# A prefetch distance of two groups for raw weights, a DRAM detour for w2, and a new order of gates, leftovers and background work

## The chip, the core and the metric

The kernel runs on one core of one Trainium2 chip. The metric is the device time of one execution in microseconds; the figure given for a kernel is the median of its runs. TensorE, VectorE (DVE), ScalarE (ACT) and GpSimd (POOL) each work through their own queue in order; nearly all DMAs are issued by SyncE (SP), whose queue is in order too.

## The reference

```python
x = delta_attention(q, k, v, beta)      # 4 batches, 8 heads, 768 steps, head size 48; gives x [3072, 384]
logits = x @ w_gate                     # [3072, 8]
P = np.exp(logits - logits.max())
for _ in range(8):                      # Sinkhorn: rows, then columns
    P /= P.sum(1, keepdims=True) + 1e-09
    P /= P.sum(0, keepdims=True) + 1e-09
    P *= N / E
for e in range(8):
    h = np.maximum(x @ w1[e], 0.0)      # w1 [8, 384, 1024], w2 [8, 1024, 384]
    out += P[:, e:e + 1] * (h @ w2[e])
h = out @ w_in                          # w_in [384, 2048] and w_out [2048, 384] arrive as 64-bit floats
result = (h * np.cos(h)) @ w_out
```

## The kernel before

Every large product is made of three TensorE passes over rounded high parts and low remainders (`hi` and `lo`; the low part is the subtraction source minus high part, on VectorE or GpSimd).

*Attention and expert 0.* 12 chunks (`tick`, orders written out by hand in `SEQ`) run the attention; between their steps `half()` runs pieces of expert 0 for the blocks of 512 tokens that are done. In the last three chunks every second step also pops one closure of `t_prog(0)`, which loads blocks of x from DRAM (`lds`), makes sums and differences of them (`ops` on GpSimd, `neg` on VectorE), splits them into high and low (`emit`) and stores them in `tsc`.

*Lead.* From line 1299 the first raw weights and the tiles T (sums of x, 15 of them, 512 KB each) are loaded, and a loop (L1340) alternates pieces of expert 0 with the lists in `lead` and with Sinkhorn steps (`sk_some`, 12 in all; each waits on TensorE for a matmul with ones and then runs some eight small VectorE operations). Six pieces of expert 0 are left over for group 0 (`LEFT`).

*Groups.* Experts 1 to 7 run in 56 calls of `group(n)`: two passes (p = 0, 1) over 1536 tokens each, 28 groups of 256 hidden columns to a pass. A group makes 6 hidden tiles of 128x512 (three token blocks, two column halves) with 15 products of three matmuls (`m`, L1425) over sums of x and sums of w1, and sums of the results (`copy` on ScalarE, L1430; `vadd` on VectorE, L1433). Five PSUM banks X, Z, A, B, C_ change roles from group to group. `relu` (ScalarE L155, then VectorE L156) writes a hidden tile. Six calls of `F()` in a group each pop one fill piece: 9 matmuls of the second layer (`seg_piece`, L149) of the pair of groups before; every fourth piece closes a token block, and the next `gates()` multiplies the three banks by the gate (VectorE, L1457) and adds them on GpSimd (L1458). `bg()` pops one closure of background work, from group 4 on: `t_prog(1)` for the second pass, then the conversion of w_in and w_out (`conv`, nine VectorE steps per slice; the next slice's load two steps before its use).

*Weights of a group.* `g_load(n + 1)` at the start of group n loads raw w1 into `wraw` (first pass), and `s_prep(n + 1)` returns seven lists that `go(0)` to `go(6)` run at set places: `q0`, `q1` make the sums on GpSimd, `hi` and `lo` split them, `g_load2` then loads w2 into the same 768 columns of `wraw`, `w2h` and `w2l` split it, and `store` writes the finished sums (1.9 MB) to `wss`. The second pass loads those from `wss` and needs raw w2 alone. The places in a group, by products and fill pieces:

```python
N0 N2 F gates go(0) bg N1 N4 bg F go(1) bg N3 gates CE b a bg CD F gates go(2) bg
DF EF CF F gates go(3) d c F gates go(4) bg e relu go(5) F gates bg go(6)
```

*End.* After group 55 eight fill pieces are left and run between the first three steps of the last network (`net_step`), whose weights are loaded into ten tiles `cw` that take the place of the tiles T.

## Time and profile before

| | us |
|---|---|
| median of 3 runs (2369.21 to 2374.89) | 2370.85 |
| the profiled execution's own time | 2375.54 |
| its span | 2373.8 |
| TensorE busy in it | 2141.5 (90%) |
| VectorE busy | 1416.0 (60%) |
| GpSimd busy | 939.2 (40%) |
| ScalarE busy | 864.3 (36%) |

The span runs from the first to the last instruction that the profiler saw. A busy time is the union of an engine's instructions. An engine's idle time is put to the instruction that ends it and to whatever released that instruction. The granted clock is TensorE's, 1.0 for 2.4 GHz and 0.5 for 1.2 GHz, averaged over a stretch.

### The profile page before, as it was taken

How to read it: one execution, taken by the hardware profiler on the slowest of the kernel's cores; microseconds unless marked ns; L12 is line 12 of the kernel's file. 1: busy time of each engine (PE TensorE's matmuls, PEld its weight loads, DVE VectorE, ACT ScalarE, POOL GpSimd, SP SyncE). 2: the span in 40 equal slices, each digit the busy share in tenths (PEclk: the TensorE clock that was granted, in tenths of full speed). 3: DMA queues.
4: the chain of work that ended last, by engine and by line, in shares of the span. 5: the costliest groups of instructions: out<-in, count | busy, mean ns of one | idle time of the engine just before them, and what ended most of it. 6: DMA issues, size and time to landing. Idle time of an engine off the chain costs nothing.

```text
span 2373.8 us, 39737 instructions
## 1 busy us (share of the span) xinstructions
PE 2141.5 (90%) x16148; PEld 1755.9 (74%) x16148; DVE 1416.0 (60%) x2226; ACT 864.3 (36%) x1436; POOL 939.2 (40%) x1034
## 2 busy tenths in 40 slices
PE   7899999778788888888897989999999999999999
PEld 6787877566666676666675767777777778999998
DVE  6665433745556666666674656666666546666665
ACT  3333322333333333333332322323333325666665
POOL 4576542244455333333343433233323333333332
PEclk6899999889999999999998999999999999999999
DMA  4433244443344343333337532433434344000000
GB/s 86 109 86 81 74 142 141 171 155 128 138 152 148 111 163 108 115 125 127 129 120 285 198 133 94 170 127 125 150 111 158 110 148 171 27 27 27 14 4 24
DMA packets 210294, 279.71 MB, mean 118 GB/s; under 512 B 85520, under 2 KB 165872, under 8 KB 210112
## 3 DMA queue, kind: packets, MB, share of 16 engines
q1 hardware_dynamic: 207280, 270.40, 34.5%
q0 software_dynamic: 1664, 6.49, 0.8%
q8 instruction: 126, 2.06, 0.3%
q10 hardware_dynamic: 1168, 0.30, 0.1%
q14 instruction: 56, 0.46, 0.1%
HBM read 176.11 MB, written 101.02 MB: 117 GB/s over the span
## 4 chain that ended last, share of the span: by engine, by line
PE 70%; DMA 10%; DVE 7%; POOL 5%; issue 3%; ACT 3%; SPq 2%; POOLq 0%; DVEq 0%; ACTq 0%
PE ps L149 26%; PE ps L1425 18%; PE ps L1689 8%; PE ps L1647 8%; DMA wraw<-in_moe_w_dram 7%; PE ps L137 4%; DVE cth L1457 1%; DMA tp<-in_moe_w_in_dram 1%; PE ps L311 1%; ACT mh L155 1%; POOL tp L1044 1%; DVE w2t L1265 1%; PE ps L279 1%; SPq L1258 1%; DVE ps L1433 1%
## 5 line engine op out<-in xcount | busy, mean ns | idle before, releaser
L149 PE MATMUL ps<-mh,w2t 128*128 128x512 f32 x3060 | 769.4, 396 | 35.5 <-DVE cth L1457 35.5
L1425 PE MATMUL ps<-T,w1t 128*128 128x512 f32 x2520 | 671.8, 408 | 142.9 <-ACT scr L1430 94.9
L149 PEld LDWEIGHTS ps<-mh,w2t 128*128 128x128 f32 x3060 | 572.3, 190 | 184.2 <-DVE cth L1457 68.7
L1425 PEld LDWEIGHTS ps<-T,w1t 128*128 128x128 f32 x2520 | 489.5, 197 | 273.5 <-ACT scr L1430 107.0
L1458 POOL TENSOR_TENSOR accp<-accp,cth 128x512 f32<-128x512 f32 x246 | 334.5, 1389 | 700.8 <-DVE cth L1457 700.8
L155 ACT ACTIVATE mh<-ps 128x512 fp32r<-128x512 f32 x340 | 202.4, 598 | 626.1 <-PE ps L1425 246.9
L156 DVE SCALAR_TENSOR_TENSOR mh<-ps,mh 128x512 fp32r<-128x512 f32 x340 | 228.6, 687 | 180.3 <-ACT mh L155 178.9
L1433 DVE TENSOR_TENSOR ps<-scr,ps 128x512 f32<-128x512 f32 x168 | 116.5, 693 | 260.4 <-ACT scr L1430 169.8
L1430 ACT ACTIVATE scr<-ps 128x512 f32<-128x512 f32 x224 | 133.4, 595 | 150.2 <-PE ps L1425 141.7
L1656 POOL TENSOR_SCALAR tp<-tp 128x512 f32<-128x512 f32 x92 | 90.8, 987 | 204.0 <-ACT tp L1655 204.0
L1457 DVE TENSOR_TENSOR cth<-ps,scr 128x512 f32<-128x512 f32 x246 | 154.0, 681 | 1.2 <-PE ps L149 1.2
L1670 DVE TENSOR_TENSOR tp<-tp,ps 128x512 f32<-128x512 f32 x96 | 66.1, 688 | 135.7 <-ACT tp L1669 135.7
L1433 DVE TENSOR_TENSOR scr<-ps,scr 128x512 f32<-128x512 f32 x112 | 76.9, 687 | 82.7 <-PE ps L1425 50.2
L137 PE MATMUL ps<-xb,w1t 128*128 128x512 f32 x432 | 116.8, 416 | 5.5 <-DVE h L156 4.1
L1249 ACT ACTIVATE w1t<-wraw 128x128 fp32r<-128x128 f32 (+2 forms) x84 | 46.7, 590 | 200.1 <-DMA wraw<-in_moe_w_dram 195.3
L149 PE MATMUL ps<-h,w2t 128*128 128x512 f32 x396 | 103.1, 407 | 0.0
L137 PEld LDWEIGHTS ps<-xb,w1t 128*128 128x128 f32 x432 | 80.6, 195 | 24.2 <-DVE h L156 4.2
L1238 POOL TENSOR_TENSOR wraw<-wraw 128x256 f32<-128x256 f32 x28 | 20.4, 728 | 195.3 <-DMA wraw<-in_moe_w_dram 180.1
L149 PEld LDWEIGHTS ps<-h,w2t 128*128 128x128 f32 x396 | 77.0, 197 | 16.9
L390 POOL TENSOR_TENSOR w1t<-w1t 128x30 f32<-128x30 f32 (+9 forms) x150 | 81.0, 540 | 11.8
L1647 PE MATMUL ps<-xx,cw 128*128 128x512 f32 x360 | 84.0, 390 | 0.0
L1252 DVE TENSOR_TENSOR w1t<-wraw,w1t 128x128 fp32r<-128x128 f32 (+2 forms) x84 | 82.4, 981 | 0.0
(280 smaller groups left out, 2819.6 us busy)
## 6 DMA issues: line engine op xcount, KB each, us to landing
wss<-w1t SPq DMA_DIRECT2D x56, 768.0 KB
w1t<-wss SPq DMA_DIRECT2D x56, 768.0 KB
wraw<-in_moe_w_dram SPq DMA_DIRECT2D x84, 384.0 KB
wsn<-tp SPq DMA_DIRECT2D x64, 192.0 KB
wss<-w1t SPq DMA_DIRECT2D x28, 384.0 KB
scr<-pts SPq DMA_DIRECT2D x42, 256.0 KB
w1t<-wss SPq DMA_DIRECT2D x28, 384.0 KB
xsc<-xb SPq DMA_DIRECT2D x24, 384.0 KB
```

The source lines that it names most:

```text
L137: nc.tensor.matmul(out=ps[:, :nn], lhsT=w[:, a, kk, fs], rhs=x[:, b, kk, c0:c0 + nn], start=(i == 0), stop=(i == 3 * KD - 1),)
L149: nc.tensor.matmul(out=banks[kd], lhsT=w[:, a, f % 2, kd * 128:(kd + 1) * 128], rhs=h[:, b, :], start=(first and b == 0 and a == 0), stop= ...
L155: nc.scalar.activation(out=h[:, 0, :nn], in_=ps[:, :nn], func=ACTF.Relu)
L156: nc.vector.scalar_tensor_tensor(out=h[:, 1, :nn], in0=ps[:, :nn], scalar=0.0, in1=h[:, 0, :nn].bitcast(F32), op0=ALU.max, op1=ALU.subtract,)
L1425: nc.tensor.matmul(out=bank, lhsT=s_of(n, nm, a), rhs=T[:, b, :], start=start and q == 0, stop=q == 2, skip_group_check=True)
L1430: nc.scalar.activation(out=out, in_=in_, func=ACTF.Copy, scale=scale)
L1433: nc.vector.tensor_tensor(out=out, in0=a, in1=b, op=op)
L1457: nc.vector.tensor_tensor(out=c, in0=yb[kd], in1=pslot[t], op=ALU.mult)
L1458: nc.gpsimd.tensor_tensor(out=a[:, kd, :], in0=a[:, kd, :], in1=c, op=ALU.add)
L1647: nc.tensor.matmul(out=hb2(i), lhsT=net_w1(f, a, kk), rhs=x2[b](c, kk), start=(j == 0), stop=(j == 3 * KD - 1))
L1656: (nc.gpsimd if i > 3 else nc.vector).tensor_scalar(out=a, in0=a, scalar1=-MAGIC, scalar2=1.0, op0=ALU.add, op1=ALU.mult)
L1689: nc.tensor.matmul(out=ybk[t][:, :DM], lhsT=h[:, a, ts], rhs=net_w2(f, c), start=(f == 0 and j == 0), stop=(f == FT2 - 1 and j == 2),)
```

## The change

- Raw w1 of a group is loaded one group earlier than before, by `raw_next` inside `go(3)`, ahead of the store, once the last slice of `wraw` is rounded. `g_load` at the start of a group is gone; in the second pass `go(0)` issues the load of the finished sums.
- w2 is first copied from DRAM to DRAM (`w2_copy`, four groups ahead, into `w2c`), then loaded by `w2_get` into the low-part half of its own tile in `go(2)`; `w2h` rounds it from there (`go(5)`) and `w2l` subtracts in place (`go(6)`). The second pass does the same in place of its load into `wraw`.
- `go(0)` stands at the very start of a group; `gates()` after the sixth fill piece stands ahead of the last relu and of `w2l`; a background slot is added after `go(3)`; background work starts at group 2 in place of 4.
- `t_prog(0)` makes its sums on VectorE; its closures are split (two sums, rounding, subtraction with stores), and its loads are issued ahead of the rounding. In `t_prog(1)` (GpSimd) two empty slots stand ahead of each step.
- Sinkhorn: five steps in the lead's loop in place of nine, after pieces 1, 2, 5, 7 and 9; the rest after each fill piece of group 0, in a bank that group 0 now leaves alone (the order of banks changes, and A and C_ share one in group 0).
- End: `net_step(0)` follows group 55 at once, the fill pieces go four by four, the first weights go into the tiles that are free first, and x2 is split before product d.

```diff
+            def gap(k=2):
+                if rest:
+                    q.extend([lambda: None] * k)
...
             def ops(*l):
-                def run():
-                    for o, a, b, *sign in l:
-                        g(out=s[o], in0=s[a], in1=s[b], op=sign[0] if sign else ALU.add)
-                q.append(run)
+                gap()
+                add = g if rest else v.tensor_tensor
+
+                def run(o, a, b, sign=ALU.add):
+                    add(out=s[o], in0=s[a], in1=s[b], op=sign)
+
+                for i in range(0, len(l), 2):
+                    q.append(lambda m=l[i:i + 2]: [run(*x) for x in m])
...
+            def both(load, *out):
+                if rest:
+                    emit(*out)
+                    lds(*load)
+                else:
+                    lds(*load)
+                    emit(*out)
...
-                g_load2(n)
...
-        def g_load2(n):
-            p, e, g = gidx(n)
-            b = w2[e, g * 256:(g + 1) * 256, :]
+        def w2_copy(r):
+            _, e, g = gidx(r)
             nc.sync.dma_start(
-                out=wraw()[:, 0:768].rearrange("p (j d) -> p j d", j=2), in_=b.rearrange("(j p) d -> p j d", p=128)
-            )
+                out=w2c[r].rearrange("p (j d) -> p j d", j=2),
+                in_=w2[e, g * 256:(g + 1) * 256, :].rearrange("(j p) d -> p j d", p=128),
+            )
+
+        def w2_get(n):
+            nc.sync.dma_start(out=w2reg(n)[:, 768:1536].bitcast(F32), in_=w2c[n % GP])
...
             def w2h():
-                nc.scalar.activation(out=w2reg(n)[:, 0:768], in_=r, func=ACTF.Copy)
+                x = w2reg(n)
+                nc.scalar.activation(out=x[:, 0:768], in_=x[:, 768:1536].bitcast(F32), func=ACTF.Copy)
...
+            def raw_next():
+                if n + 1 < GP:
+                    g_load(n + 1)
+
+            get = lambda: w2_get(n)
             if n >= GP:
-                return [[], [], [w2h], [w2l], [], [], []]
-            return [[q0, q1, hi(s_p, ps)], [lo(s_p, ps)], [hi(s_f, fs), lo(s_f, fs), lambda: g_load2(n), hi(s_u, us)],
-                    [lo(s_u, us), hi(s_v, vs)], [lo(s_v, vs), w2h], [w2l], [store]]
+                return [[lambda: g_load(n)], [], [get], [], [], [w2h], [w2l]]
+            return [[q0, q1, hi(s_p, ps)], [lo(s_p, ps)], [get, hi(s_f, fs), lo(s_f, fs), hi(s_u, us)],
+                    [raw_next, lo(s_u, us), hi(s_v, vs)], [lo(s_v, vs)], [store, w2h], [w2l]]
...
-            if nb in (1, 2, 3, 4, 5, 6, 7, 8, 9):
+            if nb in (1, 2, 5, 7, 9):
                 sk_some()
...
-        bank = [pa[2], pa[1], pa[3], pa[0], hb]
+        bank = [pa[2], pa[1], hb, pa[0], pa[3]]
...
-            for _ in range(k if gnow[0] > 3 else 0):
+            for _ in range(k if gnow[0] > 1 else 0):
...
-            if n + 1 < NGR:
-                g_load(n + 1)
+            if n == 0:
+                A = C_
+            if n + 4 < GP:
+                w2_copy(n + 4)
...
             s1 = tt[3]
+            go(0)
             m(X, "N0", True)
...
             gates()
-            go(0)
             bg()
...
             F()
-            while sk:
+            if n == 0:
                 some()
...
             go(3)
+            bg()
+            if n == NGR - 1:
+                for kd in range(KD):
+                    x2_split(0, kd)
             m(X, "d")
...
             m(Z, "e")
-            relu(n, 1, 1, Z)
             go(5)
             F()
+            while sk and n == 0:
+                some()
             gates()
+            relu(n, 1, 1, Z)
             bg()
             go(6)
-            if n == NGR - 1:
-                for kd in range(KD):
-                    x2_split(0, kd)
...
-        for g in range(5):
-            wx[g] = cw[2 * g], cw[2 * g + 1]
-        for g in range(5):
+        for g, (a, c) in enumerate(((2, 3), (4, 5), (0, 1), (6, 7), (8, 9))):
+            wx[g] = cw[a], cw[c]
             w2_load(g)
-        F()
-        F()
         net_step(0)
-        F()
-        F()
+        for _ in range(4):
+            F()
         gates()
         net_step(1)
-        F()
-        F()
+        for _ in range(4):
+            F()
+        gates()
         net_step(2)
```

## Rows read from the trace of the kernel before

**Rows 1.** The page: span and instructions.
```profile
span 2373.8 us, 39737 instructions
```

**Rows 2.** Windows: length, busy PE, PEld, DVE, ACT, POOL (count), clock, DMA share, GB/s.
```profile
395.00:440.50 45.50, 34.70 (x145) 25.34 (x144) 30.84 (x74) 12.85 (x22) 13.70 (x14) 0.92 0.70 263
440.50:470.50 30.00, 27.74 (x110) 22.18 (x109) 20.11 (x39) 13.81 (x26) 5.01 (x7) 0.89 0.23 56
470.50:1261.50 791.00, 656.58 (x2655) 513.88 (x2654) 477.85 (x732) 251.30 (x440) 336.80 (x333) 0.93 0.39 139
1261.50:1926.00 664.50, 624.77 (x2675) 499.63 (x2674) 406.25 (x640) 197.00 (x325) 227.60 (x162) 0.98 0.42 143
1926.00:1985.00 59.00, 53.58 (x233) 42.74 (x232) 27.36 (x44) 19.46 (x32) 21.87 (x19) 1.00 0.71 281
```

**Rows 3.** First copy of each group (tile ct): count, first and last start.
```profile
L1430 ACT ACTIVATE ct<-ps x28: 578/599/614, 470.7 to 1261.9; 128x512 f32<-128x512 f32 x28
...
L1430 ACT ACTIVATE ct<-ps x28: 597/599/604, 1261.9 to 1926.3; 128x512 f32<-128x512 f32 x28
...
L1430 ACT ACTIVATE ct<-ps x3: 597/599/599, 1808.8 to 1855.0; 128x512 f32<-128x512 f32 x3
...
L1430 ACT ACTIVATE ct<-ps x2: 599/599/599, 1236.2 to 1261.9; 128x512 f32<-128x512 f32 x2
```

**Rows 4.** Waits, groups 1 to 27: total us, times, longest us.
```profile
ACT w1t L1249 <- DMA wraw<-in_moe_w_dram: 195.2, 25, 14.3
...
PE ps L1425 <- ACT scr L1430: 94.2, 25, 14.3
...
PE ps L149 <- DVE cth L1457: 20.6, 13, 2.3
...
PE ps L1425 <- DVE ps L1433: 16.7, 11, 7.4
```

**Rows 5.** Waits, groups 28 to 55.
```profile
PE ps L1425 <- DVE scr L1433: 13.2, 1, 13.2
PE ps L149 <- DVE cth L1457: 12.9, 19, 0.8
PE ps L1425 <- DVE ps L1433: 12.9, 6, 7.5
```

**Rows 6.** Timeline at the start of group 20: start, us, engine, line.
```profile
1037.47 1.95 SPq L1258 DMA_DIRECT2D wss<-w1t  x3
...
1039.53 1.14 SPq L1214 DMA_DIRECT2D wraw<-in_moe_w_dram  x1
...
1047.69 0.63 ACT L1249 ACTIVATE w1t<-wraw 128x512 fp32r<-128x512 f32 x1 [12.73 <-DMA wraw<-in_moe_w_dram]
...
1048.85 0.80 PE L1425 MATMUL ps<-T,w1t 128*128 128x512 f32 x1 [6.98 <-ACT scr L1430]
```

**Rows 7.** Timeline of group 1.
```profile
477.18 0.66 SPq L1214 DMA_DIRECT2D wraw<-in_moe_w_dram  x1
...
486.16 0.63 ACT L1249 ACTIVATE w1t<-wraw 128x512 fp32r<-128x512 f32 x1 [14.32 <-DMA wraw<-in_moe_w_dram]
...
487.55 1.28 POOL L1297 TENSOR_TENSOR accp<-accp,cth 128x512 f32<-128x512 f32 x1 [38.35 <-DMA cth<-pts]
```

**Rows 8.** VectorE groups by line and shape, groups 1 to 27: busy, mean ns.
```profile
L1252 DVE TENSOR_TENSOR w1t<-wraw,w1t 128x512 fp32r<-128x512 f32 x26 | 29.2, 1125 | 0.0
...
L1252 DVE TENSOR_TENSOR w1t<-scr,w1t 128x512 fp32r<-128x512 f32 x26 | 17.6, 679 | 0.0
```

**Rows 9.** Timeline of a conversion's late load in group 32.
```profile
1388.63 0.36 DVE L1388 TENSOR_SCALAR tp<-tp 128x384 f32<-128x384 f32 x1 [9.30 <-DMA tp<-in_moe_w_out_dram]
...
1389.65 0.80 PE L1425 MATMUL ps<-T,w1t 128*128 128x512 f32 x1 [7.51 <-DVE ps L1433]
```

**Rows 10.** Waits in the lead and group 0.
```profile
PE ps L634 <- DVE small L631: 10.6, 6, 3.1
```

**Rows 11.** Waits of TensorE at the end of the attention.
```profile
PE ps L524 <- DVE Bs L479: 5.1, 1, 5.1
```

More of the change, by code (lines that the diff above doesn't have):

```diff
@@ L77 @@
     tsc = [dram.tile([15, 128, 2, 512], F32, name=f"tsc{p}") for p in range(NB // 3)]
+    w2c = [dram.tile([128, 2 * DM], F32, name=f"w2c{r}") for r in range((E - 1) * FT // 2)]
     wss = [dram.tile([128, 3840], F32, name=f"wss{r}") for r in range((E - 1) * FT // 2)]
@@ L1055, in emit @@
             def emit(nm, i, hi, also=None):
+                gap()
                 def run():
-                    nc.scalar.activation(out=s[hi].bitcast(F32R), in_=s[i], func=ACTF.Copy)
                     v.tensor_tensor(out=s[i].bitcast(F32R), in0=s[i], in1=s[hi], op=SUB)
@@ L1062, in run, with put @@
                         keep(*also)
+                    if not rest:
+                        put()
+                q.append(lambda: nc.scalar.activation(out=s[hi].bitcast(F32R), in_=s[i], func=ACTF.Copy))
                 q.append(run)
-                flush()
-            def flush():
-                def run():
-                    for o, i in later:
-                        nc.sync.dma_start(out=o, in_=i)
-                    later.clear()
-                q.append(run)
+                if rest:
+                    q.append(put)
+            def put():
+                for o, i in later:
+                    nc.sync.dma_start(out=o, in_=i)
+                later.clear()
+            def both(load, *out):
+                if rest:
+                    emit(*out)
[3 more added lines that the diff above has]
+                    emit(*out)
             lds((A_, 1, 0, 0), (E_, 1, 0, 1), (B_, 0, 1, 0), (F_, 0, 1, 1))
@@ L1078, in t_prog @@
             neg(F_, E_, B_)
-            emit("N3", F_, U_, ("CD", E_))
-            lds((C_, 2, 1, 0), (D_, 2, 1, 1))
+            both(((C_, 2, 1, 0), (D_, 2, 1, 1)), "N3", F_, U_, ("CD", E_))
             ops((C_, C_, D_), (C_, C_, B_))
             neg(D_, C_, A_)
-            emit("N4", D_, V_, ("CE", C_))
-            lds((F_, 0, 0, 0), (U_, 0, 0, 1))
+            both(((F_, 0, 0, 0), (U_, 0, 0, 1)), "N4", D_, V_, ("CE", C_))
             ops((F_, F_, U_), (A_, F_, A_, SUB), (F_, F_, E_))
-            emit("a", F_, U_, ("d", A_))
-            lds((D_, 1, 1, 0), (V_, 1, 1, 1))
+            both(((D_, 1, 1, 0), (V_, 1, 1, 1)), "a", F_, U_, ("d", A_))
             ops((D_, D_, V_), (B_, D_, B_, SUB), (D_, D_, C_))
@@ L1091, in t_prog @@
                 ops((E_, E_, C_))
-                q.append(lambda: keep("CF", E_))
-                flush()
+                q.append(lambda: [keep("CF", E_), put()])
                 return q
@@ L1299 @@
         g_load(0)
+        w2_copy(0)
         for a in range(2):
@@ L1328 @@
         sq = s_prep(0)
-        lead = [[], [], sq[0][:2], sq[0][2:] + sq[1], sq[2][3:] + sq[3][:1],
+        lead = [[], [], sq[0][:2], sq[0][2:] + sq[1], sq[2][:1] + sq[2][3:],
                 [lambda: x2sum(1), lambda: x2sum(0), lambda: tadd("CE", 1, ALU.subtract), lambda: tadd("CD", 0, ALU.subtract)],
-                sq[2][:3] + sq[3][1:] + sq[4][:1],
-                [lambda: x2sum(2), lambda: tadd("d", 0), lambda: tadd("e", 1)], sq[4][1:] + sq[5] + sq[6]]
+                sq[2][1:3] + sq[3][:1] + sq[3][1:],
+                [lambda: x2sum(2), lambda: tadd("d", 0), lambda: tadd("e", 1)], sq[4] + sq[5] + sq[6]]
         nb = 0
@@ L1349 @@
                 x()
+        for r in range(1, 4):
+            w2_copy(r)
         cv = []
@@ L1557, in group @@
             F()
+            if n == 0:
+                some()
             gates()
@@ L1570, in group @@
             F()
+            if n == 0:
+                some()
             gates()
@@ L1578, in group @@
             F()
+            if n == 0:
+                some()
             if n == 1:
@@ L1584, in group @@
             m(Z, "e")
-            relu(n, 1, 1, Z)
             go(5)
             F()
+            while sk and n == 0:
+                some()
             gates()
+            relu(n, 1, 1, Z)
             bg()
             go(6)
-            if n == NGR - 1:
-                for kd in range(KD):
-                    x2_split(0, kd)
         accb, x2, wx = {}, {}, {}
@@ L1789 @@
         cwp.tile([128, 136], F32, name="cpad")
-        for g in range(5):
-            wx[g] = cw[2 * g], cw[2 * g + 1]
-        for g in range(5):
+        for g, (a, c) in enumerate(((2, 3), (4, 5), (0, 1), (6, 7), (8, 9))):
+            wx[g] = cw[a], cw[c]
             w2_load(g)
-        F()
-        F()
         net_step(0)
-        F()
-        F()
+        for _ in range(4):
+            F()
         gates()
         net_step(1)
-        F()
-        F()
+        for _ in range(4):
+            F()
+        gates()
         net_step(2)
-        F()
-        F()
-        gates()
         cw += [wtile(x) for x in ("w1", "w1", "w1", "w2", "w2", "w2")]
```

9 lines of the change are left out of this document (4 added, 5 removed).

## The prediction

> **What bounds the kernel now.** I read the page first for the span [rows 1] and then a table by stage for TensorE's busy time and clock [rows 2] (lead, group 0, first pass, second pass, turn to the last network): in every stage it is the busiest engine, so time can come only from what it idles and from its clock. Three stages have nearly full matmul queues but different paces: the second pass over the tokens (groups 28 to 55) runs 2675 recorded matmuls in 664.5 us at a mean granted clock of 0.98; the first pass (groups 1 to 27) runs nearly the same 2655 in 791.0 us at 0.93. The starts of the groups give the same per group [rows 3]: 27 intervals in 791.2 us are 29.3 us each, 27 in 664.4 us are 24.6 us, and an undisturbed pair of the second pass takes 46.2 us, 23.1 us each. The matmuls of both passes are alike, 99 to a group. What the first pass has and the second has not is the making of the seven sums of w1 from the raw weights.
>
> In the first pass TensorE stands idle 791.0 - 656.6 = 134.4 us [rows 2]. The list of waits names who ended it [rows 4]: 94.2 us end with a ScalarE copy of a PSUM bank (`copy`, L1430), 20.6 us with the gate multiplications (L1457), 16.7 us with a VectorE sum (L1433). The ScalarE copy was itself late only because the rounding of raw w1 (`hi`, L1249) stood ahead of it in ScalarE's queue and waited for its DMA: 195.2 us. One place in order of time shows why [rows 6]: SyncE issues the 1.9 MB store of the finished sums at 1037.5, the raw load of the next group at 1039.5, and the load lands 8.2 us later, at 1047.7, whereupon TensorE has stood for 6.98 us. The buffer `wraw` holds w1 and then w2 of one group, so the load cannot start before the low half of w2 (`w2l`, L1265) is read, at the end of the group before. That is the limit: not bandwidth (DMA share 0.39 in this stage), but one buffer, and a consumer a few microseconds behind its load. The clock is a second loss: TensorE is busy 656.6 us for 2655 matmuls here, 624.8 us for 2675 there [rows 2], some 32 us more for the same work at the lower granted clock.
>
> **The change, part by part.** *Raw w1 two groups ahead, w2 into its own tile.* With w2 landing in the high-numbered half of its own tile, `wraw` is free when the last w1 slice is rounded, in the middle of the group. `raw_next` then issues the load ahead of this group's store, some 27 matmuls before the group's end (products c, d, e and fill pieces 5 and 6): at 23.1/99 us each that is 6.3 us before its new first reader, plus about 1 us in which ScalarE's copies are not yet missed. The load needed 8.2 us behind a store [rows 6]; without one it should just arrive. So nearly all of the 94.2 us goes, and with it most of the clock loss. Price: 28 more copies of 384 KB from DRAM to DRAM. The trace has none; below, nothing, since they are issued four groups ahead and no engine waits for them; above, one raw load's time in the queue, 8.2 us, in each group, which would bring the raw wait back (rival 2). I take nothing, as the queue is 0.39 busy, and keep the other end for the range. `w2_get` is issued after fill piece 3 and read after product e, 36 matmuls or 8.4 us later: about the slowest load seen, so also just in time.
>
> *Gates ahead of the last relu and of w2l.* TensorE's next fill piece overwrites the banks that the gates read. Moving two VectorE operations behind them removes the 20.6 us here and the 12.9 us of the second pass (19 times about 0.68 us, once in a pair of groups) [rows 4, 5]. The undisturbed pace becomes 23.1 - 0.68/2 = 22.8 us.
>
> *What is late next in the first pass.* (a) Weight conversion: its load is issued two slots before VectorE needs it, and behind a transfer of 1.9 MB it comes late (9.30 us of VectorE, 7.51 us of TensorE [rows 9]). In the second pass such waits cost TensorE the 12.9 us on L1433 beside the 13.2 us of the turn [rows 5], over some 20 conversions; the shorter first pass has 12 of its own, beside stores of the same size: 10 us (7 to 25). (b) The VectorE sum A is due one microsecond after product N3; of its 16.7 us the longest wait, 7.4, comes from a late copy [rows 4], so 9 us stay; VectorE is busy 477.9/27 = 17.7 us of a group, 78% of the shorter one. I take 10. (c) Start: the Sinkhorn steps end in group 0 instead of its first third, so the gates' table reaches DRAM behind the store of group 1, the multiplication `acc_mul` waits on GpSimd for it (38.35 us now [rows 7]), and its slot makes SyncE wait ahead of `w2_get`. The 14.32 us of group 1 go (its raw load is already there), but I leave 13 us: one late load of 8.2 us and two of 2 to 3. (d) Clock: 33 us of stalls for 134 leave a quarter of the 32 us: 8. Sum: 27 x 22.8 = 616, plus 10 + 10 + 13 + 8 = 657 us, 134 less than now (110 to 165).
>
> *Second pass.* Minus 12.9 for the gates. The 13.2 us at the turn remain in the main (15 tiles of 512 KB are loaded there whatever the order); w2h is moved 36 matmuls later, so that ScalarE no longer waits there first, worth 3. Together -15 (-25 to 0: the background slots come at other places, and 12.9 us of conversion waits can come out twice as large or nil).
>
> *Lead.* Four of ten Sinkhorn steps leave it and the rest are spread; TensorE waited 10.6 us for them [rows 10]. Each carries some 3.3 us of VectorE work into group 0, where VectorE is busy 20.1 of 30.0 us [rows 2], so it fills group 0 and gives part back: -4 (-10 to +5).
>
> *First sums on VectorE, background split up.* 14 sums in the attention leave GpSimd; the one long stall seen there is 5.1 us [rows 11], and the loads now run ahead of the rounding: -2 (-5 to +5; VectorE can now wait for those loads itself). Split and padded background work starts at group 2 with 8 slots a group: 104 steps + 291 of conversion = 395, in 50 groups, so it ends by group 52 and nothing is left for the last one: nothing (otherwise its remnant, about 0.5 us a step).
>
> *End.* Stage idle is 59.0 - 53.6 = 5.4 us [rows 2]; splitting x2 before product d and loading the first weights into tiles that are free earlier hides most: -4 (-5 to +4).
>
> **Sum.** -134 - 15 - 4 - 2 - 4 = -159 from the profiled execution's 2375.5 us: 2216.5; this execution stands 4.7 us above the median of the runs, so 2212 us. Bounds of the parts: -210 to -96, thus 2161 to 2275.
>
> **A rule beside a row.** The same subtraction of 128x512 took 1125 ns on the mean while GpSimd made its sums, and 679 ns later in the group [rows 8]. So VectorE work that meets GpSimd is dearer, and the forecast has the sums of the next group at the very start, beside the gates. The Trainium skill, SBUF — State Buffer, "Who interferes with whom", says that a VectorE instruction with two SBUF inputs contends with a GpSimd instruction that reads SBUF, and that the later one waits for the whole instruction. The row agrees in direction. By that rule all five low halves of a group would be stretched, VectorE would come near to its limit, and the outcome would be rival 1.
>
> **Rivals.** *1. VectorE and ScalarE become the limit in the first pass.* For it: 78% busy, in-order, dearer beside GpSimd. Against: the second pass runs free at 61% with the same critical sums. Price: the groups stay at the 25.7 us of a group whose raw load was nearly in time [rows 3]: 27 x 25.7 + 13 = 707, 50 more than 657: 2262 us. *2. The load still comes late in every second group*, because `w2_get`, the copy and conversion traffic stand in front of it on SyncE's queue. 13 groups x (5 us + 1.2 of clock) = 80: 2292 us. For it: a margin of 7.3 us against 8.2 and 9.0 seen. Against: no store ahead any more. *3. Slower.* `w2_get` holds ScalarE: everything behind w2h (last relu, next copies) waits with it. It decides from the point where the load lands more than 8.4 + 5.9 = 14.3 us after issue in every group (29.3 - 657/27 = 5.0 of the first pass, 25/27 = 0.9 of the rest). At 15.5 us in all 27 it is 2212 + 27 x 7.1 = 2404 us. Against: the two slowest raw loads read here took 8.2 and 9.0 us [rows 6, 7]. *4. The raw load is not what is waited for*: SyncE, in order, is held by a conversion store or a table load before it comes to `raw_next`, and only the gates gain: about 2345 us. *5. Everything hides*: the first pass at 22.8 with 15 us of stalls: 2185 or less.
>
> **Chances.** Forecast (2180 to 2250): 0.60; rival 1: 0.17; rival 2: 0.11; rival 3: 0.04; rival 4: 0.03; rival 5 below 2180: 0.05. The range reaches over rival 1 and half of rival 2 and most of rival 5: 2165 to 2285. Faster by over 0.3% (7 us; about what a measurement here can tell from no change): 0.95; within: 0.01; slower: 0.04.
>
> **What the profile would show.** Right: no wait of ScalarE on raw w1 in the first pass; group starts 24 to 24.5 us apart; granted clock there 0.97 or more; no TensorE wait on L1457. Wrong: ScalarE waiting at w2h or the first rounding (rival 2 or 3), sum A waited for in every group (rival 1), a tall stall in groups 1 to 3 beyond 13 us, conversion loads above 25 us, or background steps left before the last group.

## The result and the profile after

The changed kernel takes 2165.27 us (median of 4 runs, 2161.86 to 2167.82) against 2370.03 on the same chip: a ratio of 0.9134, 95% interval 0.9111 to 0.9158. The forecast was 2212: the median lies below the 2180 to 2250 to which it gave a chance of 0.60, where only rival 5 (0.05) stood, and at the edge of the wider range of 2165 to 2285. The profiled execution has these first lines on its page (busy us, share of the span, instructions):

```profile
span 2161.4 us, 39859 instructions
...
PE 2074.3 (96%) x16147; PEld 1738.0 (80%) x16147; DVE 1447.3 (67%) x2240; ACT 860.5 (40%) x1436; POOL 934.1 (43%) x1020
```

The span is 212.4 us shorter than that of [rows 1]. The same stages as in [rows 2], now for the changed kernel (length, busy time and count by engine, clock, DMA share, GB/s):

```profile
382.70:421.50 38.80, 32.18 (x139) 23.99 (x137) 22.10 (x44) 13.71 (x24) 16.18 (x16) 0.91 0.86 317
421.50:455.50 34.00, 28.60 (x111) 22.06 (x112) 28.15 (x67) 12.89 (x25) 7.45 (x12) 0.90 0.35 128
455.50:1100.50 645.00, 613.57 (x2656) 499.05 (x2656) 486.56 (x712) 246.68 (x438) 339.81 (x327) 0.98 0.52 182
1100.50:1720.50 620.00, 609.85 (x2673) 502.12 (x2673) 420.88 (x663) 197.68 (x325) 231.25 (x163) 0.99 0.44 153
1720.50:1780.00 59.50, 59.50 (x272) 50.30 (x271) 32.87 (x52) 23.65 (x39) 24.41 (x22) 1.00 0.73 278
```

TensorE's idle time in the first pass fell from 134.4 us to 31.4, in the second from 39.7 to 10.2, and its busy time in the first pass from 656.6 to 613.6 for the same matmuls. Most of that is the clock, 0.98 instead of 0.93: at a granted clock of 0.5, 154 matmuls started later than 227 ns after one another, by 33.0 us in all; now it is 19 and 4.2 us. The first copy of each group gives the starts, as in [rows 3]:

```profile
L1458 ACT ACTIVATE ct<-ps x28: 578/590/602, 455.5 to 1100.7; 128x512 f32<-128x512 f32 x28
...
L1458 ACT ACTIVATE ct<-ps x28: 590/598/602, 1100.7 to 1720.8; 128x512 f32<-128x512 f32 x28
```

Measured between the same marks, forecast and outcome stand so:

| stage | before | after | change | forecast |
|---|---|---|---|---|
| to the attention's last eviction | 395.4 | 382.7 | -12.7 | -2 |
| lead and group 0 | 75.3 | 72.8 | -2.5 | -4 |
| groups 1 to 27 | 791.1 | 645.1 | -146.0 | -134 |
| second pass, 27 intervals | 664.5 | 620.2 | -44.3 | -15 |
| start of group 55 to the end | 447.4 | 440.6 | -6.8 | -4 |
| sum | | | -212.3 | -159 |

TensorE's waits in groups 1 to 27, and ScalarE's on the two loads (total us, times, longest), the answer to [rows 4]:

```profile
ACT w2t L1281 <- DMA w2t<-w2c: 21.1, 2, 19.4
...
PE ps L1453 <- ACT ct L1458: 16.5, 2, 16.4
...
ACT w1t L1268 <- DMA wraw<-in_moe_w_dram: 9.6, 6, 2.1
...
PE ps L1453 <- DVE w1t L1271: 5.4, 7, 1.1
PE ps L1453 <- ACT scr L1458: 4.7, 2, 2.6
PE ps L1453 <- DVE ps L1461: 4.5, 6, 1.2
```

ScalarE's 195.2 us on raw w1 are 9.6, and the gates' line (20.6 us) is gone. One wait of 16.4 us holds half of what is left. In the second pass, the answer to [rows 5]:

```profile
PE ps L1453 <- DVE ps L1461: 9.5, 4, 6.0
...
PE ps L150 <- DVE cth L1485: 0.3, 1, 0.3
```

The 13.2 us of the turn are not there at all. SyncE's queue around the start of a group shows the new order, the answer to [rows 6]:

```profile
902.31 0.38 SPq L1230 DMA_DIRECT2D wraw<-in_moe_w_dram  x1
...
911.96 1.91 SPq L1277 DMA_DIRECT2D wss<-w1t  x3
```

and ScalarE's queue there the rounding that reads this load, with no wait at its end (a wait would stand in brackets):

```profile
912.27 0.62 ACT L1268 ACTIVATE w1t<-wraw 128x512 fp32r<-128x512 f32 x1
```

The load has 10 us and the store goes after it. The tall wait is in group 1, the answer to [rows 7]; SyncE's part of the timeline first:

```profile
469.58 15.14 SPq L1317 DMA_DIRECT2D cth<-pts  x2
484.82 0.46 SPq L1242 DMA_DIRECT2D w2t<-w2c  x1
```

ScalarE's timeline there:

```profile
491.37 0.84 ACT L1281 ACTIVATE w2t<-w2t 128x768 fp32r<-128x768 f32 x1 [19.42 <-DMA w2t<-w2c]
```

TensorE's:

```profile
493.75 2.93 PE L1453 MATMUL ps<-T,w1t 128*128 128x512 f32 x6 [16.38 <-ACT ct L1458]
```

And GpSimd's:

```profile
480.63 3.70 POOL L1322 TENSOR_TENSOR accp<-accp,cth 128x512 f32<-128x512 f32 x3 [23.58 <-DMA cth<-pts]
```

The second table waits for the slot of the first, SyncE stands for 15.14 us, and w2's load behind it comes late to ScalarE, whose copies TensorE needs.

### The profile page after: what moved, and what is told of

Same layout as the page of the kernel before. It is cut to its first block, busy times and chain, and to the rows that moved or that the text cites. A ratio compares the mean times of both kernels' runs of the same rounds, so it can differ in the third digit from the quotient of the medians.

```text
span 2161.4 us, 39859 instructions
## 1 busy us (share of the span) xinstructions
PE 2074.3 (96%) x16147; PEld 1738.0 (80%) x16147; DVE 1447.3 (67%) x2240; ACT 860.5 (40%) x1436; POOL 934.1 (43%) x1020
## 4 chain that ended last, share of the span: by engine, by line
PE 80%; DVE 8%; DMA 5%; POOL 3%; issue 2%; SPq 1%; ACT 1%; DVEq 0%; POOLq 0%; ACTq 0%
PE ps L150 30%; PE ps L1453 22%; PE ps L1726 9%; PE ps L1684 9%; PE ps L138 4%; DMA tp<-in_moe_w_out_dram 1%; DVE w1t L1271 1%; DVE cth L1485 1%; PE ps L312 1%; DVE mh L157 1%; DMA cth<-pts 1%; DMA T<-xsc 1%; POOL w1t L391 1%; PE ps L280 1%; POOL w1t L387 1%
## 5 line engine op out<-in xcount | busy, mean ns | idle before, releaser
L150 PE MATMUL ps<-mh,w2t 128*128 128x512 f32 x3060 | 750.8, 390 | 0.5 <-DVE cth L1485 0.3
L1453 PE MATMUL ps<-T,w1t 128*128 128x512 f32 x2520 | 642.1, 394 | 46.4 <-DVE ps L1461 17.3
L1453 PEld LDWEIGHTS ps<-T,w1t 128*128 128x128 f32 x2520 | 474.0, 190 | 157.8 <-DVE ps L1461 23.9
L1461 DVE TENSOR_TENSOR ps<-scr,ps 128x512 f32<-128x512 f32 x168 | 116.6, 694 | 114.3 <-PE ps L1453 95.0
L1461 DVE TENSOR_TENSOR scr<-ps,scr 128x512 f32<-128x512 f32 x112 | 76.9, 687 | 72.0 <-PE ps L1453 60.7
L150 PEld LDWEIGHTS ps<-h,w2t 128*128 128x128 f32 x396 | 75.3, 193 | 16.1
L1257 POOL TENSOR_TENSOR wraw<-wraw 128x256 f32<-128x256 f32 x28 | 29.9, 1068 | 127.4 <-DMA wraw<-in_moe_w_dram 92.4
L1692 ACT ACTIVATE tp<-ps 128x512 f32<-128x512 f32 x96 | 56.2, 586 | 63.8 <-PE ps L1684 63.8
L387 POOL TENSOR_TENSOR w1t<-Nsys,w1t 128x30 f32<-128x30 f32 (+9 forms) x150 | 76.5, 510 | 11.4
```

Of the source, the lines that this page charges most:

```text
L150: nc.tensor.matmul(out=banks[kd], lhsT=w[:, a, f % 2, kd * 128:(kd + 1) * 128], rhs=h[:, b, :], start=(first and b == 0 and a == 0), stop= ...
L1453: nc.tensor.matmul(out=bank, lhsT=s_of(n, nm, a), rhs=T[:, b, :], start=start and q == 0, stop=q == 2, skip_group_check=True)
L1461: nc.vector.tensor_tensor(out=out, in0=a, in1=b, op=op)
```

## Experiments

All medians are beside the changed kernel's 2165; the letters are the theories of the expectation above each result. Passes are given as the 27 intervals of [rows 3] (after: 645.1 and 620.2).

### The two passes

**Gates alone**, on the kernel before: gates ahead of the last relu and of `go(5)`.

```diff
             m(Z, "e")
-            relu(n, 1, 1, Z)
-            go(5)
             F()
             gates()
+            relu(n, 1, 1, Z)
+            go(5)
```

> The kernel before with one edit: after product e the sixth fill piece and the gates come first, then the last relu and w2l. Theory W (the second pass gained mainly from the later place of w2h): the gates give about 1.3 us a pair of groups, 17 us in the second pass and 15 to 30 in the first, where the raw wait takes part of it back: about 2330 us. Theory G (the gates gave most of the second pass's 44 us, the term was only read too low): 40 us in the second pass and 25 or more in the first: 2305 us or less.

2330.84 us (2367.16 for before there), ratio 0.9852 (0.9837 to 0.9867): passes 775.6 (-15.5) and 641.7 (-22.8). The time is W's, not G's; W gave the second pass 17, G 40. The second pass alone gives more than its whole forecast of 15, from the gates' place only (`go(5)` has an empty list there). TensorE's waits in it:

```profile
PE ps L1425 <- DVE scr L1433: 13.0, 2, 12.8
...
PE ps L149 <- DVE cth L1457: 2.4, 4, 0.8
```

The gates' 12.9 us of [rows 5] are 2.4; the turn's stall, 13.2 there, stays.

**Gates left behind**, in the changed kernel.

```diff
             m(Z, "e")
+            relu(n, 1, 1, Z)
             go(5)
             F()
...
+            go(6)
             gates()
-            relu(n, 1, 1, Z)
             bg()
-            go(6)
```

> The changed kernel with the gates after the sixth fill piece behind the last relu and behind w2l again, everything else as changed. Theory G (the gates' move is worth what the waits of before showed, 20.6 us in the first pass and 12.9 in the second): TensorE waits for the gates' multiplications some 19 times for 0.7 us in each pass, undisturbed pairs of the second pass 45.5 to 46.2 us instead of 44.8; time 2185 to 2195 us. Rival H (with w2l behind it on VectorE, which itself waits for ScalarE's rounding of w2, the gates come much later than before the change, and the first pass pays 2 us and more in every second group): 2200 to 2230 us. Rival W (it was w2's rounding that made the gates late, so with that moved the gates cost nothing where they stand): 2163 to 2170 us.

2214.17 us, 49 more: passes 673.0 (+27.9) and 639.5 (+19.4). TensorE's waits on the gates in the first pass:

```profile
PE ps L150 <- DVE cth L1485: 38.7, 14, 17.9
```

And in the second pass:

```profile
PE ps L150 <- DVE cth L1485: 10.1, 14, 1.6
```

The time is H's; W, by which the gates would cost nothing here, falls. In the first pass a gate costs 27.9/14 = 2.0 us by the time, as H says. By the list it is 20.8/13 = 1.6 without the start's 17.9, which was ScalarE's 16.4 in the changed kernel (group 1 lasts 36.9 us, there 37.6). In the second pass the waits are G's 0.7 us, but the groups that carry one last 23.7 us instead of 22.4. A wait that the list prices at 0.7 us costs 1.3.

**w2 rounded early** in the second pass: load, rounding and subtraction in the second to fourth lists.

```diff
-                return [[lambda: g_load(n)], [], [get], [], [], [w2h], [w2l]]
+                return [[lambda: g_load(n)], [get], [w2h], [w2l], [], [], []]
```

> The changed kernel, but in the second pass w2_get, w2h and w2l at the places of before (go(1), go(2), go(3)). Theory W: ScalarE waits for w2 in the middle of a group again, above all at the turn between the passes (about 13 us) and in every fourth group (1 to 2 us each): 20 to 28 us slower than the changed kernel, about 2190 us. Theory G: within 4 us of the changed kernel.

2190.32 us, and the second pass lasts 647.4 (+27.2), the first 646.4. W holds. Waits of its second pass:

```profile
ACT w2t L1281 <- DMA w2t<-w2c: 49.8, 12, 10.7
...
DVE scr L1461 <- ACT scr L1458: 44.5, 11, 10.8
...
PE ps L1453 <- ACT scr L1458: 14.2, 4, 6.5
```

The same chain is in the kernel before, where the prediction did not follow it. ScalarE's waits in groups 28 to 55 there:

```profile
ACT w2t L1261 <- DMA wraw<-in_moe_w_dram: 39.3, 9, 13.1
```

The timeline of ScalarE at the turn:

```profile
1286.33 0.84 ACT L1261 ACTIVATE w2t<-wraw 128x768 fp32r<-128x768 f32 x1 [13.09 <-DMA wraw<-in_moe_w_dram]
```

And that of TensorE:

```profile
1288.51 2.92 PE L1425 MATMUL ps<-T,w1t 128*128 128x512 f32 x6 [13.18 <-DVE scr L1433]
```

TensorE resumes 2.2 us after the rounding of w2 begins. The 13.2 us that [rows 5] puts to a VectorE sum are w2's.

**Raw load behind the store**, in the sixth list instead of the fourth.

```diff
-                    [raw_next, lo(s_u, us), hi(s_v, vs)], [lo(s_v, vs)], [store, w2h], [w2l]]
+                    [lo(s_u, us), hi(s_v, vs)], [lo(s_v, vs)], [store, raw_next, w2h], [w2l]]
```

> The changed kernel, but the raw load of w1 is issued right behind the store of the finished sums (go(5)) in place of go(3). Theory P (the load's place ahead of the store is what the first pass gained by): the load lands some 8 us after the end of the group, TensorE stands 5 to 7 us in each of 27 groups and the granted clock falls: 2290 to 2360 us. Rival (w2 out of the raw buffer and the other moves are enough): under 30 us slower, below 2195 us.

2293.39 us: first pass 765.4 (+120.3), second 621.3. P holds. In the first pass:

```profile
ACT w1t L1268 <- DMA wraw<-in_moe_w_dram: 152.7, 26, 12.0
...
PE ps L1453 <- ACT ct L1458: 119.3, 26, 22.8
```

SyncE, in order, issues the load only when the store is out, and the store waits for VectorE's low halves; its waits in the first pass, and its timeline at one place:

```profile
SPq L1277 <- DVE w1t L1271: 197.6, 32, 20.7
```

```profile
918.86 3.45 SPq L1277 DMA_DIRECT2D wss<-w1t  x3
922.41 0.74 SPq L1230 DMA_DIRECT2D wraw<-in_moe_w_dram  x1
```

**Raw load in the same list, but ahead of the store.**

```diff
-                    [raw_next, lo(s_u, us), hi(s_v, vs)], [lo(s_v, vs)], [store, w2h], [w2l]]
+                    [lo(s_u, us), hi(s_v, vs)], [lo(s_v, vs)], [raw_next, store, w2h], [w2l]]
```

> The changed kernel with the raw load of the next group moved from the fourth list to the sixth, as in the earlier run (2293 us), but issued ahead of the group's store. It then has about one fill piece, the last relu and w2's rounding, some 3 us, until ScalarE's first rounding of it, where the load took 8.2 us behind a store. Theory T (the time between issue and first reader decides): it still comes 4 to 6 us late in every group, so that the first pass stays at 730 to 770 us: 2255 to 2293 us. Rival Q (the 1.9 MB ahead of it in the queue were what made it late): without them it lands within 4 us, first pass 650 to 690 us: 2170 to 2210 us.

2190.17 us, first pass 668.4 (+23.3). Rival Q: ScalarE waits 43.2 us in 11 groups in place of 152.7 in 26. In SyncE's timeline at the start of a group the load is issued here:

```profile
906.24 0.38 SPq L1230 DMA_DIRECT2D wraw<-in_moe_w_dram  x1
```

Its reader in ScalarE's timeline:

```profile
910.09 0.63 ACT L1268 ACTIVATE w1t<-wraw 128x512 fp32r<-128x512 f32 x1 [3.03 <-DMA wraw<-in_moe_w_dram]
```

Of the 120 us, 97 are the store ahead in the queue and 23 the later list. But the list is not the time of issue, and the load is not as late here as behind the store. In groups 2 to 25 SyncE issued it 12.2 us after the first copy of a group in the changed kernel (median), 12.9 here, and 21.8 behind the store. So theory T was not put to the test as meant, and the 97 us are in the main an issue held up by a store that waits for its data. The transfer itself is a smaller part: where ScalarE waited for the load, it was with its reader 3.8 to 6.7 us after issue here (median 4.5) and 3.9 to 8.0 behind the store (5.8).

**Each copy of w2 made twice**, `w2d` being a tensor that nothing reads.

```diff
-            nc.sync.dma_start(
-                out=w2c[r].rearrange("p (j d) -> p j d", j=2),
+            for c in (w2d, w2c):
+                nc.sync.dma_start(
+                    out=c[r].rearrange("p (j d) -> p j d", j=2),
```

> The changed kernel with each of the 28 copies of w2 from DRAM to DRAM made twice, the additional one into a tensor that nothing reads. Theory H (the copies are hidden; SyncE and the queue have room at those places): 2162 to 2169 us. Rival K (a copy costs about its share of the queue in the first pass, 8.2 us at most in each group, because the raw load or w2's load behind it come late): 2180 us or more, with waits of ScalarE for raw w1 or w2 in many groups in place of 9.6 us in six.

2168.45 us (2166.31 to 2173.75), passes 648.2 and 620.2; DMA share 0.55 instead of 0.52. H: hidden, 3 us at most for 28 more copies.

**Conversion half a group later.**

```diff
-        bgq.extend(cv)
+        bgq.extend([lambda: None] * 4 + cv)
```

> The changed kernel with four empty background slots ahead of the conversion of the last weights, so that every conversion load and store falls at another place of a group (half a group later). In the changed kernel conversion waits cost TensorE about 4.5 us in the first pass and 9.5 in the second; the forecast gave 10 and 12.9. Theory L (where these loads fall against the other transfers decides, so the low value is luck of the place): the sum of the waits on a VectorE sum changes by more than 8 us, time 2172 to 2185 us. Rival D (the loads have slack wherever they stand, since the queue in a pass is about half busy): 2162 to 2169 us.

2183.39 us, 18 more, 13.6 of it in the second pass. L: the changed kernel's few conversion waits are a matter of place. Nearly all lies in one, at the turn; VectorE's timeline:

```profile
1124.06 0.36 DVE L1416 TENSOR_SCALAR tp<-tp 128x384 f32<-128x384 f32 x1 [14.46 <-DMA tp<-in_moe_w_out_dram]
```

TensorE's:

```profile
1125.08 2.93 PE L1453 MATMUL ps<-T,w1t 128*128 128x512 f32 x6 [13.96 <-DVE ps L1461]
```

### The start

**Tables issued by GpSimd**, in `acc_mul`:

```diff
             b, z = 3 * p + t, ctile(3)
-            nc.sync.dma_start(
+            nc.gpsimd.dma_start(
```

> The changed kernel, but the gate tables of acc_mul are loaded on GpSimd's DMA queue in place of SyncE's. Theory Z (the 16.4 us that TensorE stands between groups 1 and 2 is SyncE held by the second of these loads, with w2_get and the raw load behind it): 13 to 17 us faster than the changed kernel, about 2150 us. Rival (the transfers themselves are late, behind store and accumulator loads): the wait stays over 10 us and the time within 5 us of the changed kernel.

2170.55 us; Z's time fell, and the rival's is passed by 0.3 us. Group 1 shrinks from 37.6 to 27.7 us, but group 2 grows from 26.9 to 36.1. The edit moves the second pass's tables too: its group 31 grows from 22.5 to 29.0 us. GpSimd's queue:

```profile
475.77 3.72 POOL L1322 TENSOR_TENSOR accp<-accp,cth 128x512 f32<-128x512 f32 x3 [14.52 <-DMA accp<-ysc]
479.79 0.79 POOL L1317 DMA_DIRECT2D cth<-pts  x1 [0.29 <-POOL accp L1322]
489.23 3.78 POOL L1322 TENSOR_TENSOR accp<-accp,cth 128x512 f32<-128x512 f32 x3 [8.66 <-DMA cth<-pts]
493.31 0.78 POOL L1317 DMA_DIRECT2D cth<-pts  x1 [0.29 <-POOL accp L1322]
498.53 3.72 POOL L1322 TENSOR_TENSOR accp<-accp,cth 128x512 f32<-128x512 f32 x3 [4.44 <-DMA cth<-pts]
...
505.86 0.72 POOL L1257 TENSOR_TENSOR wraw<-wraw 128x256 f32<-128x256 f32 x1
```

Now GpSimd waits for the first partial output and then for the second and third table, and the sums of w1 for group 3 stand behind all three.

**Three slots for the tables.**

```diff
-            b, z = 3 * p + t, ctile(3)
+            b, z = 3 * p + t, ctile(3 if p else None)
```

> The changed kernel with the three gates' tables of the first acc_mul in three different slots, so that SyncE no longer waits for GpSimd to read one before it may issue the next. Changed kernel on record: 2165 us, groups 0, 1, 2 last 33.9, 37.6, 26.9 us. Theory Z (the one late slot holds SyncE, and all that stands behind it comes late): the load of w2 of group 1 is issued some 14 us earlier, groups 1 and 2 last 25 and 24 us, 15 us less: about 2150 us. Rival C (the chain on GpSimd is as long as before: the first multiplication still waits until about 480 us for its data, then nine of 1.25 us, then the gates' additions, and only then the sums of w1 for the next group): group 1 shrinks to about 26 us but group 2 stays at 31 to 34 us, because ScalarE's rounding waits for GpSimd's sums: 2158 to 2163 us.

2165.03 us, groups 1 and 2 at 34.0 and 30.0. SyncE no longer stands there, and nothing is won. That is C's mechanism in part: the time missed its range by 2 us, and group 1 did not come down to C's 26. Now the gates wait for the slots too. TensorE's waits from 418 to 545 us:

```profile
PE ps L150 <- DVE cth L1485: 17.6, 3, 12.0
```

**Three slots, partial outputs loaded in group 0** and no longer behind it.

```diff
             go(3)
+            if n == 0:
+                for t in range(3):
+                    acc_load(0, t)
```

> The same three slots, and the three loads of the first partial outputs (768 KB each, issued after group 0 and ahead of the tables) moved into group 0, after its fourth list. Theory C (GpSimd's chain of data, multiplications and gates sets the start): the first multiplication starts some 8 to 10 us earlier, at about 471 us instead of 480.6, so the sums of group 2 are no longer late and groups 1 and 2 come to about 25 and 24 us: 2148 to 2152 us. Rival (the tables, not the partial outputs, are late, since the Sinkhorn steps end only in group 0): the multiplication starts no earlier than 478 us, and the time is within 3 us of the kernel with three slots alone. Bad case: 2.3 MB more in the queue during group 0 makes its own loads late, group 0 grows from 33.9 to 38 us or more.

2157.24 us (2152.94 to 2161.52), groups 1 and 2 at 28.4 and 30.4: the first multiplication now starts 22.2 us after group 1 (27.3 with the slots alone). That is 5 us above C's forecast; GpSimd still does nine multiplications in a row, which the next run undoes.

**One slot, multiplications spread** over groups 1 and 2, on top of the early loads; `acc_tab` is the load of `acc_mul`, `acc_do` its multiplications.

```diff
@@ after the first piece
             if n == 1:
                 acc_mul(0, 0)
+            if n == 2:
+                acc_do(1)
@@ after the second
-            if n == 1:
-                acc_mul(0, 1)
+            if n == 2:
+                acc_tab(0, 2)
@@ after the fifth
             if n == 1:
-                acc_mul(0, 2)
+                acc_tab(0, 1)
+            if n == 2:
+                acc_do(2)
```

> The kernel with the early loads of the partial outputs, but with one slot for the tables again and the three multiplications spread: the first table and its multiplication in group 1; the second table loaded at the end of group 1 and multiplied early in group 2, behind that group's sums of w1; the third loaded in group 2 and multiplied at its end. The kernel with early loads stands at 2157 us, with groups 1 and 2 at 28.4 and 30.4 us. Theory C (what is left of the start is GpSimd's nine multiplications in a row ahead of the gates' additions and the sums of w1, and the gates that wait for the tables' slots): groups 1 and 2 last 23 to 25 us each, about 10 us less: 2146 to 2149 us. Rival N (the stall only moves on to group 3, whose gates wait for the third multiplication): groups 1 to 3 together no more than 4 us shorter than there (81.2 us): 2153 to 2158 us.

2146.50 us, groups 1 to 3 at 23.7, 23.6, 21.5: C. The start is mended, 19 us below the changed kernel.

**Spread, and one slot more for a conversion's load.**

```diff
         cv.append(lambda a=o[8], b=st_: [a(), b()])
+        cv.extend([lambda: None] * (i < 28))
```

> The same as the spread kernel, and one empty background slot between a conversion's store and the next one's first VectorE step for the first 28 of the 32 conversions, so that a conversion's load has three slots of time in place of two. Shifting all of them by half a group had cost 18 us, nearly all in one wait of 14.5 us at the turn. Theory L (a conversion load that is slower than its two slots is the only stall left in the second pass, 9.5 us, and some of the first): TensorE's wait for VectorE sums falls below 4 us over both passes, 6 to 10 us less than the spread kernel: about 2140 us. Rival P (the few late loads stand behind whole groups' transfers and are late by more than a slot, and the new places meet other transfers): within 5 us of the spread kernel on either side, or up to 15 us above it if one meets the turn.

2134.09 us, 0.9003 (0.8985 to 0.9022): L, by more than forecast. All of TensorE's waits in its second pass:

```profile
PE ps L1461 <- DVE scr L1469: 2.1, 2, 2.0
```

The pass takes 608.2 us, 22.5 a group. This version beats both kernels, the changed one by 31 us.

### Lead, attention, end

**Nine Sinkhorn steps in the lead again.**

```diff
-            if nb in (1, 2, 5, 7, 9):
+            if nb in (1, 2, 3, 4, 5, 6, 7, 8, 9):
```

> The changed kernel with nine Sinkhorn steps in the loop of the lead, as before the change, in place of five. Lead and group 0 together last 38.9 + 33.9 = 72.8 us in the changed kernel and 45.5 + 29.8 = 75.3 us in the one before; the forecast gave the spreading 4 us. Theory K (spreading the steps is what saves those 2.5 us): lead and group 0 together come back to about 75 us; the rest is as it was: 2167 to 2169 us. Rival T (with the steps done early, the gates' tables reach DRAM early, and the stall of group 1 shrinks by more than the lead loses): lead and group 0 about 75 us, groups 1 and 2 together 52 to 58 us in place of 64.5: 2157 to 2163 us.

2185.58 us, outside both. `some()` loads the three tables each time it finds no step left, so it issued twelve loads, which held SyncE; group 0 took 48.5 us. This run says nothing on the question.

**The same, tables loaded once.**

```diff
         def some():
+            if not sk:
+                return
             sk_some()
```

> Nine Sinkhorn steps in the loop of the lead again, as in the earlier run, but with the loads of the gates' tables issued once, when the last step is done. In the earlier run twelve such loads, nine of them superfluous, held SyncE for 27.7 us of group 0. Theory K (spreading the steps saves what lead and group 0 gained): lead and group 0 together 75 to 76 us in place of 72.8, groups 1 and 2 as in the changed kernel: 2167 to 2169 us. Rival T (tables that reach DRAM some 10 us earlier shorten group 1, whose first multiplication waits for its table): groups 1 and 2 together below 60 us in place of 64.5: 2158 to 2163 us.

2159.84 us (2159.47 to 2161.81), 5 below the changed kernel. K is right on lead and group 0 (75.5 us), T on the time: groups 1 and 2 last 53.4 us in place of 64.5. GpSimd's first multiplication comes 12.4 us after group 1 begins at 464.7, where it came 25.1 after 455.5:

```profile
477.08 4.52 POOL L1322 TENSOR_TENSOR accp<-accp,cth 128x512 f32<-128x512 f32 x3 [9.15 <-DMA cth<-pts]
```

**First sums of x on GpSimd again.**

```diff
-                add = g if rest else v.tensor_tensor
+                add = g
```

> The changed kernel with the first sums of x back on GpSimd, nothing else undone. Before the lead the changed kernel is 12.7 us ahead (last eviction of the attention's last step at 382.7 us against 395.4), where the forecast gave 2. Theory S (the sums on VectorE are what shortens the last three attention steps, since there GpSimd was late): the last eviction comes 5 to 8 us later, and the time is 2170 to 2174 us. Rival Q (splitting the closures and issuing the loads ahead of the rounding did it, or the slow-clock warm-up at the start, which was 7 us shorter in that execution): 2163 to 2168 us, last eviction within 2 us of 383 us for the same warm-up.

2165.86 us. S fell. The eleventh attention step (between ScalarE's evictions of the transposed x) takes 32.0 us; it took 40.0 before and 32.3 after.

**Loads behind the rounding again.**

```diff
-                if rest:
-                    emit(*out)
-                    lds(*load)
-                else:
-                    lds(*load)
-                    emit(*out)
+                emit(*out)
+                lds(*load)
```

> The changed kernel with the loads of the first sums of x issued behind the rounding and its stores again, as before the change; the sums stay on VectorE and the closures stay split. The eleventh step of the attention lasted 40.0 us before and 32.4 us after (between the ScalarE evictions of the transposed x), and putting the sums back on GpSimd left it at 32.0. Theory O (the loads' place is what took out the 18.0 us wait of GpSimd for one load and the VectorE and TensorE waits behind it): the eleventh step comes back to 37 to 40 us: 2170 to 2174 us. Rival U (the splitting of the closures did it, since one closure no longer holds VectorE for three sums and a rounding): the step stays at 32 to 33 us: 2163 to 2168 us.

2168.29 us, the step 34.2 us: below O's 37 to 40. Other runs whose attention has the loads ahead show 30.5 to 34.2 us for the same step, so the loads' place shows no effect. By exclusion the 6 to 10 us are the splitting of the closures, U's cause, which was not undone by itself.

**End as before**: weights in rising order, leftover pieces in twos around the three steps, `x2_split` behind the last `go(6)`.

```diff
-        for g, (a, c) in enumerate(((2, 3), (4, 5), (0, 1), (6, 7), (8, 9))):
-            wx[g] = cw[a], cw[c]
+        for g in range(5):
+            wx[g] = cw[2 * g], cw[2 * g + 1]
...
-        for _ in range(4):
-            F()
+        F()
+        F()
...
```

> The changed kernel with the end as before: the last network's first weights into tiles in rising order, the leftover pieces in twos between its steps, and the splitting of x2 behind the last group. From the start of the last group to the end the changed kernel takes 440.6 us against 447.4 before; the forecast gave 4. Theory E (the end's own edits are worth all of it): that stretch comes back to 446 to 448 us, time 2171 to 2173 us. Rival B (a part of it comes from the last group itself, which has no more conversion or gates to wait for): 442 to 445 us, time 2166 to 2169 us.

2171.10 us, the last stretch 446.1 us: E, 5.5 of the 6.8 us.

## Why the prediction was right in direction and too small

**The step that failed** is the second pass: "The 13.2 us at the turn remain in the main (15 tiles of 512 KB are loaded there whatever the order); w2h is moved 36 matmuls later, so that ScalarE no longer waits there first, worth 3. Together -15". Measured: -44.3. Undone by themselves, w2's place costs 27.2 us and the gates 19.4, 46.6 together. The wait was read at its last link, a VectorE sum at the turn, and given to the tiles loaded there. Followed two links further, it was ScalarE's rounding of w2, in nine groups and 39.3 us, the turn's 13.1 among them. The gates were mis-sized: 12.9 us of listed waits were taken as the price, where each lengthens its pair by 1.3 us, not 0.68. That the time came out where rival 5 put it is not rival 5's doing: its first pass of 631 us or less measured 645.1.

**First pass.** The mechanism held: the raw load early and ahead of the store is worth 120.3 us, the gates 27.9. What w2's own tile gives there by itself was not undone. The margin was read too narrowly on both sides. The 8.2 us behind a store are near the top of the 25 late loads of the kernel before, which ran from 3.1 to 9.0 us. The new load is issued 9.7 us (median of groups 2 to 25) before its reader, not 6.3: SyncE is ahead of the engines and waits at this load mostly for the buffer (for VectorE's low halves, 71.2 us in 16 waits). In the six groups where it still comes late it had 5.4 to 6.7 us. The four terms for what is late next came to 41 us as a sum; measured, 645.1 - 27 x 22.4 = 40.3. That the sum fits is luck, for they were wrong one by one: conversion and sum A together 4.5 us on L1461 instead of 20; the clock 4.2 instead of 8; the start (groups 1 to 3: 37.6 + 26.9 + 22.4 - 67.2) 19.7 instead of 13, with the one tall stall of 16.4 us that the prediction named as a sign of being wrong. It had no term for the low halves of w1, for which TensorE waited 5.4 us (L1271). The 12 us between -134 and -146 are the pace, 22.4 us a group instead of 22.8, once more the gates' price. 22.4 us is TensorE's own: 99 matmuls that start 227 ns apart.

**Sinkhorn.** The forecast gave spreading the steps 4 us. It gives lead and group 0 2.7 us and lengthens groups 1 and 2 by 11, since the tables come later: a loss of 5 us by the medians, 8 by these stages, with the right mechanism named under (c) but not set against the lead's gain. **Attention.** 5.1 of the 12.7 us are there at the fifth of the twelve steps' marks, before the changed code, and lie within what executions differ in (below); 7.7 are the eleventh step, of whose stall of 5.1 the forecast took 2. The twelfth step gives 1.7 back: 24.0 us in every run with the changed kernel's attention, 22.3 before. **Copies.** A second set costs 3 us at most; the forecast took nothing for the first. **End.** 5.5 us instead of 4.

**Rivals.** VectorE is not the limit: 486.6 us busy in 645, and undisturbed groups run at TensorE's pace. The subtraction of [rows 8] beside GpSimd's sums still took 902 ns on the mean against 697 later:

```profile
L1271 DVE TENSOR_TENSOR w1t<-wraw,w1t 128x512 fp32r<-128x512 f32 x26 | 23.5, 902 | 0.0
...
L1271 DVE TENSOR_TENSOR w1t<-scr,w1t 128x512 fp32r<-128x512 f32 x26 | 18.1, 697 | 0.0
```

The rule of the Trainium skill, SBUF — State Buffer, "Who interferes with whom", agrees with these rows in direction again but didn't decide. The raw load is late in six groups by 9.6 us in all, not in every second; w2's load holds ScalarE once, for 19.4 us. SyncE held by a table load (the fourth rival's mechanism) is real, but in one group. That rival's price, 2345, does not follow from its own condition: 2371 less the gates' 33.5 is 2337, and the gates alone measured 2331.

## What to carry to other kernels

Follow a wait back until it reaches a load or an instruction that waited for nothing: the list names only the last link, and the group it names need not be the cause. Look at what stands ahead of a load on an in-order DMA queue, and at what that waits for: in the same list the load cost 97 us more behind a store that waited for its data. When one edit defers small steps, look at what reads their result, and price that with the gain.

## What the runs showed of the hardware

- Where ScalarE waited for it, a raw load of 384 KB was with its reader 3.1 to 9.0 us after issue in the kernel before, 3.9 to 8.0 in the run behind the store and 3.8 to 6.7 in the run ahead of it. A gates' table of 256 KB, which reads the same 2 KB for all 128 partitions, took 9.4 us (479.79 to 489.23 in the run with tables on GpSimd's queue) and the next one 5.2 (493.31 to 498.53). What sets these times stayed open.
- A listed TensorE wait of 0.65 us behind a gate cost 1.2 us (second pass of the run with the gates behind): the matmul started 1.04 us after the one before it in place of 0.227, and the next five started 255 to 343 ns apart, 0.4 us more. The groups were 1.3 us longer.
- TensorE ran 41 to 61 us of the first 120 at half clock (1.2 GHz), differing between kernels with the same code there, and the mark of the third step fell between 116.8 and 122.1 us. A difference of 5 us ahead of the lead is no finding.
